# A four-batch attention and token-mixing kernel: another written-down order, split first reads, and Strassen pieces of 384 and 160 columns

## The chip, the cores and the metric

The kernel runs on one core of one Trainium2 chip. The core has five engines that run their own instruction streams in order and meet only at semaphores: TensorE (PE: matrix products and transposes), VectorE (DVE), ScalarE (ACT), GpSimd (POOL) and SyncE (SP), which here only starts transfers. Transfers are moved by 16 DMA engines; an engine that starts one spends some time on issuing it. The metric is the device time of one execution in microseconds (us), the median over several executions. Before the change it is 234.49 us (three runs, 233.85 to 238.21).

## The reference: what is computed

Two blocks follow each other, for a batch of B = 4, H = 4 heads, S = 1088 positions and head dimension D = 32, so that the model width is H*D = 128.

```python
def phi(x):                                   # r = 8 sketch directions
    a = np.einsum('rd,bhsd->bhsr', S1, x)
    b = np.einsum('rd,bhsd->bhsr', S2, x)
    return np.einsum('bhsi,bhsj->bhsij', a, b).reshape(*x.shape[:-1], r * r)
q_p, k_p = phi(q), phi(k)
kv  = np.einsum('bhsf,bhsd->bhfd', k_p, v)
num = np.einsum('bhsf,bhfd->bhsd', q_p, kv)
den = np.einsum('bhsf,bhf->bhs', q_p, k_p.sum(axis=2))[..., None] + 1e-6
x = num / den                                 # then heads side by side: (B, S, 128)
theta = x @ w_theta
zr, zi = x * np.cos(theta), x * np.sin(theta)
y = np.einsum('ts,bsd->btd', w_tok_r, zr) + np.einsum('ts,bsd->btd', w_tok_i, zi)
u = x + y
out = u + np.maximum(u @ w_ch, 0.0)
```

S1 and S2 are 8 x 32, w_theta and w_ch 128 x 128; these and the two 1088 x 1088 token matrices arrive as 64-bit floats and are turned into 32-bit ones on the chip. The denominator can come near zero, which is why the kernel works with split numbers (a rounded part and a rest) where the queries and keys meet.

## The kernel before

**Work per batch.** The 1088 positions are padded to nine chunks of 128, handled in three groups of three (384 columns). For the keys: the sum of squares on ScalarE (L676) sets a rounding step; VectorE writes the keys rounded to it (L700) and the rest of the subtraction (L705); TensorE forms the 32 x 32 second moments of rounded part and rest (L711 to L752). Beside this, `kfeatures` (L756) transposes the keys group by group (L779, the operation at L781), forms both sketches with the small matrix `sbk`, multiplies them out on VectorE and sums them against v. `chain` (L824) then turns the second moments into a small scaled matrix for the denominator: `split` on VectorE, an addition on ScalarE (L839), a product on TensorE (`first`, operands sq and sf), a split and a scaling (L867), a second product (operand pbd), and a row of some eleven tiny VectorE steps (`cut`) that ends in `mv` and `mf`. `levels` (L1020) multiplies the transposed queries with them (`exact` with 16-bit operands, `whole` with 32-bit ones), and VectorE makes the denominators. `outputs_x` (L1075) makes the attention output x, its angles and z, the 17 blocks of 128 rows (real and imaginary) that are mixed. The chains run for batch 0, batch 1, and batches 2 and 3 together.

**Mixing.** The token matrices come as 17 rows of 128 x 1088 64-bit numbers (1088 KB each). `weight` (L631) reads one into one of five buffers of class zs, makes two passes on ScalarE (L638, L640), and a shift and a combination on VectorE (L642, L644, the latter the custom operation on 128 x 2176 16-bit words). Batches 0 and 1 multiply every row by z directly, in pieces of 384, 384 and 320 columns (`mix_row`, L1208). Batches 2 and 3 are done together by Strassen's scheme (`winograd`, L1248): seven products of eight matmuls, each over half the positions (HT = 544 columns) that are cut into the pieces of PARTS (L149). The additions of rows that the scheme needs run on VectorE (asum 1 and 2) and on GpSimd (asum 3 and 4, in 16 operations of 128 x 544).

**End of a piece.** `finish` (L1234) multiplies u by w_ch on TensorE, adds the positive part on VectorE (L1238), transposes on VectorE (L1239) and stores the piece with four transfers, one for each 32 columns of the output, on SyncE's queue (L1241 to L1246).

**What sets the order.** No scheduler decides at build time. All operations are recorded first, each with its engine, its buffers and its readers and writers. Then `ORDER` (L34) gives the sequence in which they are issued, and `STARTS` (L79) a time for each. `run` (L245) uses the times to give buffers their slots, and `issue` (L264) uses them for one more thing: ahead of a TensorE operation it puts idle matmuls into TensorE's stream (`spin`, 128 x 384 with 16-bit operands), five for each microsecond that the written times leave between two TensorE operations:

```python
for _ in range(int((o.start - last - 0.08) * FILL)):
    fill()
```

Each engine then works through its own part of the order and waits wherever an operand or a buffer isn't ready. Besides these, 39 short idle matmuls of 112 columns open TensorE's stream (L430). Small transfers have no queue of their own: `read_heads` (L440) reads the two sketch matrices into the four heads' partitions, two of the four copies on ScalarE's queue and two with S2 alone on SyncE's, ahead of the keys.

Of the kernel before, what the change touches and what calls it, by code (L numbers as in the profile page):

```python
# [34 lines left out]
    4, 2, 5, 6, 0, 1, 3, 33, 30, 35, 7, 31, 8, 340, 137, 11, 9, 350, 12, 37, 13, 36, 14, 132, 34, 10, 21, 136, 335,  # L35
    48, 95, 138, 125, 96, 52, 370, 250, 53, 97, 15, 54, 49, 16, 231, 345, 251, 89, 232, 141, 142, 143, 254, 90, 119,
    17, 252, 55, 98, 133, 126, 56, 256, 57, 58, 59, 120, 60, 61, 62, 63, 64, 65, 26, 101, 75, 99, 66, 67, 144, 145,
    91, 102, 257, 50, 134, 76, 233, 18, 341, 77, 92, 139, 342, 140, 27, 78, 343, 42, 351, 68, 51, 69, 32, 70, 28, 71,
    19, 72, 255, 103, 344, 73, 227, 74, 121, 79, 29, 228, 93, 80, 243, 104, 244, 229, 81, 22, 352, 303, 82, 305, 122,
    353, 375, 83, 304, 20, 84, 41, 123, 161, 23, 146, 307, 85, 354, 86, 306, 308, 113, 87, 147, 234, 162, 336, 148,  # L40
    237, 114, 371, 127, 309, 88, 179, 163, 238, 245, 128, 310, 198, 420, 253, 423, 164, 180, 129, 421, 109, 424, 202,
    338, 135, 426, 425, 105, 427, 108, 44, 239, 43, 373, 428, 365, 315, 204, 422, 259, 258, 39, 94, 246, 191, 240,
    429, 346, 311, 430, 260, 100, 115, 45, 316, 431, 312, 106, 348, 376, 185, 432, 149, 150, 207, 46, 186, 433, 107,
    187, 230, 116, 337, 378, 151, 152, 153, 313, 434, 117, 154, 355, 261, 155, 314, 156, 262, 157, 158, 203, 159, 435,
    110, 192, 160, 436, 367, 193, 165, 181, 372, 437, 111, 438, 347, 112, 360, 118, 317, 263, 124, 439, 130, 166, 380,
    194, 167, 182, 208, 357, 446, 440, 442, 168, 188, 447, 441, 449, 131, 209, 453, 169, 443, 170, 450, 374, 448, 319,
    47, 456, 454, 318, 457, 199, 451, 455, 200, 377, 458, 171, 349, 444, 459, 390, 320, 339, 476, 445, 172, 452, 264,
    265, 361, 173, 468, 460, 478, 210, 470, 266, 267, 211, 268, 212, 269, 462, 270, 271, 461, 205, 356, 526, 174, 520,
    272, 463, 395, 366, 235, 523, 24, 527, 464, 175, 471, 521, 465, 479, 201, 25, 466, 241, 524, 176, 472, 469, 528,
    467, 40, 213, 236, 206, 525, 273, 274, 275, 242, 358, 522, 276, 485, 381, 529, 379, 480, 482, 359, 486, 474, 473,  # L50
    363, 391, 487, 530, 475, 277, 481, 362, 368, 488, 531, 410, 247, 177, 364, 214, 215, 278, 477, 489, 532, 392, 369,
    385, 490, 483, 396, 533, 178, 534, 491, 383, 382, 195, 405, 492, 384, 535, 386, 183, 323, 493, 324, 189, 285, 387,
    494, 536, 388, 400, 537, 321, 389, 248, 407, 216, 184, 38, 217, 218, 219, 190, 538, 220, 397, 221, 196, 484, 222,
    223, 224, 495, 393, 286, 415, 546, 225, 322, 394, 401, 549, 547, 226, 398, 197, 496, 402, 539, 249, 283, 548, 399,
    542, 284, 406, 287, 540, 288, 497, 550, 553, 289, 551, 541, 408, 556, 552, 403, 290, 543, 557, 404, 568, 544, 291,
    325, 554, 545, 292, 498, 409, 555, 417, 293, 560, 558, 562, 412, 499, 570, 563, 559, 299, 571, 411, 294, 660, 326,
    654, 576, 564, 561, 565, 413, 661, 572, 414, 655, 573, 657, 566, 658, 578, 567, 416, 500, 656, 418, 574, 579, 577,
    631, 419, 580, 632, 582, 633, 662, 585, 659, 569, 663, 501, 664, 665, 575, 608, 508, 586, 666, 581, 514, 634, 667,
    502, 609, 515, 279, 584, 329, 668, 296, 587, 669, 635, 670, 327, 509, 588, 671, 636, 295, 672, 589, 687, 610, 280,
    583, 611, 673, 516, 612, 281, 688, 590, 282, 328, 300, 297, 330, 637, 298, 613, 503, 680, 614, 517, 615, 842, 331,  # L60
    689, 332, 333, 591, 690, 691, 638, 334, 719, 616, 840, 725, 518, 720, 681, 519, 722, 721, 726, 674, 692, 723, 727,
    839, 617, 724, 592, 693, 728, 639, 729, 301, 675, 730, 731, 640, 676, 677, 618, 732, 678, 679, 593, 733, 302, 641,
    734, 619, 735, 594, 736, 694, 737, 682, 738, 642, 683, 752, 684, 696, 620, 685, 739, 595, 686, 702, 697, 745, 698,
    740, 699, 704, 596, 746, 741, 742, 643, 700, 705, 644, 743, 759, 744, 695, 747, 701, 597, 748, 749, 753, 621, 750,
    751, 706, 763, 844, 622, 843, 765, 710, 766, 845, 754, 712, 708, 713, 623, 755, 756, 767, 598, 818, 772, 645, 774,
    599, 768, 775, 600, 776, 707, 510, 777, 799, 757, 800, 758, 714, 703, 760, 624, 646, 761, 808, 601, 511, 771, 647,
    709, 762, 780, 801, 715, 764, 790, 648, 802, 769, 781, 778, 770, 819, 783, 791, 836, 803, 841, 773, 809, 784, 602,
    792, 779, 785, 793, 603, 787, 711, 512, 820, 649, 837, 513, 625, 847, 786, 804, 716, 821, 848, 717, 856, 805, 868,
    822, 857, 846, 806, 894, 865, 823, 858, 849, 850, 870, 851, 810, 718, 852, 807, 782, 896, 504, 788, 885, 869, 859,
    626, 794, 838, 795, 895, 866, 886, 853, 811, 824, 871, 825, 789, 796, 897, 860, 797, 861, 887, 873, 854, 862, 936,  # L70
    812, 798, 855, 863, 874, 902, 604, 971, 505, 888, 872, 876, 930, 864, 898, 605, 813, 606, 912, 877, 506, 814, 934,
    650, 913, 900, 815, 651, 867, 878, 899, 889, 875, 879, 816, 932, 890, 880, 817, 901, 933, 891, 652, 892, 653, 903,
    937, 828, 881, 829, 904, 939, 893, 507, 882, 931, 914, 941, 915, 883, 607, 954, 938, 884, 905, 935, 627, 945, 940,
    946, 830, 972, 955, 831, 956, 947, 942, 916, 826, 957, 827, 958, 944, 628, 948, 906, 943, 949, 959, 917, 832, 918,
    833, 960, 961, 950, 962, 951, 629, 919, 834, 630, 907, 984, 967, 952, 968, 908, 973, 985, 953, 909, 969, 974, 970,
    920, 975, 921, 963, 976, 835, 964, 977, 965, 978, 910, 966, 979, 911, 926, 922, 986, 923, 980, 927, 987, 924, 981,
    928, 982, 929, 988, 983, 989, 990, 994, 925, 991, 995, 992, 996, 993, 997, 998, 999, 1000, 1001,
)
STARTS = (  # L79
    90, 92, 103, 103, 130, 170, 220, 228, 274, 318, 360, 364, 389, 408, 454, 473, 473, 499, 510, 544, 560, 588, 592,  # L80
    622, 634, 648, 693, 742, 750, 764, 766, 782, 799, 872, 885, 893, 910, 924, 925, 988, 1016, 1019, 1030, 1034, 1036,
    1067, 1082, 1098, 1132, 1134, 1136, 1143, 1146, 1151, 1171, 1185, 1201, 1203, 1217, 1218, 1249, 1250, 1251, 1253,
    1255, 1257, 1257, 1259, 1261, 1263, 1265, 1278, 1284, 1305, 1296, 1330, 1355, 1368, 1381, 1383, 1398, 1403, 1417,
    1442, 1460, 1461, 1476, 1477, 1478, 1544, 1587, 1589, 1602, 1664, 1678, 1712, 1718, 1726, 1734, 1755, 1750, 1768,
    1771, 1781, 1783, 1795, 1807, 1808, 1816, 1834, 1835, 1846, 1876, 1914, 1965, 1963, 2007, 2028, 2031, 2042, 2043,
    2064, 2107, 2118, 2130, 2134, 2146, 2166, 2164, 2199, 2256, 2258, 2270, 2271, 2292, 2292, 2307, 2315, 2323, 2341,
    2369, 2397, 2412, 2410, 2421, 2445, 2448, 2496, 2510, 2542, 2560, 2545, 2575, 2568, 2607, 2622, 2678, 2717, 2731,
    2758, 2792, 2794, 2826, 2827, 2827, 2866, 2871, 2881, 2890, 2894, 2930, 2988, 2998, 2998, 3011, 3022, 3076, 3085,
    3113, 3134, 3141, 3171, 3178, 3181, 3202, 3218, 3246, 3253, 3265, 3288, 3302, 3309, 3330, 3335, 3359, 3346, 3347,
    3361, 3382, 3406, 3405, 3409, 3428, 3439, 3458, 3489, 3491, 3536, 3525, 3537, 3546, 3586, 3616, 3613, 3635, 3661,  # L90
    3678, 3711, 3713, 3720, 3745, 3745, 3774, 3784, 3799, 3802, 3812, 3827, 3841, 3879, 3886, 3892, 3912, 3905, 3942,
    3962, 3950, 3968, 3970, 3975, 3977, 3984, 3986, 3992, 3995, 4024, 4030, 4038, 4050, 4070, 4078, 4089, 4108, 4145,
    4171, 4199, 4213, 4285, 4305, 4309, 4318, 4323, 4350, 4343, 4382, 4384, 4410, 4416, 4419, 4433, 4441, 4456, 4464,
# [52 lines left out]
KEEP_CLS = "big"  # L146
PAIR = (2, 3)
QUADS = (2, 3)
PARTS = ((0, 288), (288, 544))  # L149
APOOL = ("4", "3")  # L150
KDMA = (False, True, True, True)
RDMA = (False,) * 4
# [24 lines left out]
class Layout:  # L177
# [17 lines left out]
    def buf(self, cls, shape, dt, name):  # L195
        b = Buf(cls, shape, dt, name)
        self.bufs.append(b)
        return b
# [1240 lines left out]
```

## Time and profile before

| | |
|---|---|
| median of three runs | 234.49 us (233.85 to 238.21) |
| the profiled execution's own time | 235.7 us |
| its span (first to last instruction) | 233.9 us |
| mean granted TensorE clock | 0.963 |
| PE busy | 222.1 us (95%), 2407 instructions |
| PE weight loads | 169.6 us (72%) |
| DVE busy | 178.9 us (76%), 364 |
| ACT busy | 112.8 us (48%), 239 |
| POOL busy | 54.5 us (23%), 99 |
| HBM read / written | 28.07 MB / 2.23 MB |
| share of the chain that ended last | PE 85%, ACT 5%, DVE 3%, DMA 2% |

A matmul with 32-bit operands appears as two records in the trace. Ends of matmuls are modelled, so a busy PE isn't a PE at its peak; the granted clock tells at which speed it streams. A line number in a row is that of the code before the change; L375, L379, L382 and L395 are helpers that many places call, so such rows are told apart by their tiles (ps is PSUM, big, zs, g, sm and hf are classes of buffers).

### The profile page before, as it was taken

Reading aid. Unit: us, or ns where it says so; the run is one execution under the profiler, and the core shown is the slowest. Engines: PE = TensorE matmul, PEld = TensorE weight load, DVE = VectorE, ACT = ScalarE, POOL = GpSimd, SP = SyncE. Lnnn points to the kernel's source line nnn. Section 1 sums busy time; section 2 is a strip of 40 time slices with the busy share of each in tenths; the row PEclk is TensorE's granted clock in tenths of the full one; section 3 lists DMA queues with packets and bytes.
Section 4 is the critical chain, followed back from the end, with each engine's and each line's share of the span. In section 5 each row is a group of like instructions: output and inputs, shape, how many; then the busy total and the mean of one; then the engine's idle time right before and its main releaser. Section 6 shows DMA issues by size and latency. Waiting matters only on the chain.

```text
span 233.9 us, 5837 instructions
## 1 busy us (share of the span) xinstructions
PE 222.1 (95%) x2407; PEld 169.6 (72%) x2407; DVE 178.9 (76%) x364; ACT 112.8 (48%) x239; POOL 54.5 (23%) x99
## 2 busy tenths in 40 slices
PE   7887999999999999999999999999999999999990
PEld 7665789877785667577766676677788878788770
DVE  3797586899999999999798789892678697534451
ACT  3895673999997647859842131555640000000000
POOL 1089052000470000001043000000025527980000
PEclk9999656999999999999999999999999999999996
DMA  4999999869585869400012210000051200522243
GB/s 143 417 406 300 423 416 379 317 252 425 204 296 123 304 247 308 181 0 4 0 28 34 36 28 3 3 3 4 0 72 23 34 3 0 87 35 33 43 72 54
DMA packets 24586, 33.55 MB, mean 143 GB/s; under 512 B 19184, under 2 KB 19952, under 8 KB 22384
## 3 DMA queue, kind: packets, MB, share of 16 engines
q1 hardware_dynamic: 23168, 30.29, 38.1%
q0 software_dynamic: 1296, 2.88, 6.1%
q8 instruction: 19, 0.31, 0.5%
q14 instruction: 7, 0.06, 0.1%
q10 hardware_dynamic: 96, 0.01, 0.0%
HBM read 28.07 MB, written 2.23 MB: 130 GB/s over the span
## 4 chain that ended last, share of the span: by engine, by line
PE 85%; ACT 5%; DVE 3%; DMA 2%; issue 2%; SPq 1%; DVEq 0%; ACTq 0%
PE ps L395 76%; ACT big L640 2%; PE ps L779 2%; PE ps L1005 2%; DMA big<-k_l 2%; PE ps L427 2%; PE ps L1151 2%; PE ps L1118 1%; DVE big L375 1%; ACT big L676 1%; ACT g L782 1%; DVE g L1239 0%; DVE big L382 0%; DVE g L375 0%; ACT g L1122 0%
## 5 line engine op out<-in xcount | busy, mean ns | idle before, releaser
L395 PE MATMUL ps<-big,zs 128*128 128x384 f32 (+3 forms) x380 | 112.8, 437 | 0.0
L395 PEld LDWEIGHTS ps<-big,zs 128*128 128x128 f32 x380 | 69.7, 190 | 27.0 <-DVE mv L379 0.6
L375 POOL TENSOR_TENSOR big<-big,big 128x544 f32<-128x544 f32 x16 | 22.4, 1420 | 13.3 <-PE ps L395 8.6
L640 ACT ACTIVATE big<-zs 128x1088 int32<-128x1088 uint32 (+1 forms) x18 | 21.2, 1196 | 4.8 <-DVE big L375 2.5
L638 ACT ACTIVATE big<-zs 128x1088 f32<-128x1088 f32 x17 | 21.0, 1234 | 4.7 <-DMA zs<-w_tok 3.8
L395 PE MATMUL ps<-big,big 128*32 128x32 f32 (+2 forms) x352 | 23.2, 234 | 0.0
L375 DVE CUSTOM_DVE_ANT_0 big<-big,big 128x2176 uint16<-128x2176 uint16 x17 | 21.8, 1290 | 0.1
L395 PEld LDWEIGHTS ps<-big,big 128*32 128x32 f32 (+1 forms) x352 | 16.7, 125 | 3.3 <-issue 0.3
L389 POOL DMA_DIRECT2D g<-big x6 | 5.3, 940 | 55.7 <-ACT g L1228 55.7
L427 PE MATMUL ps<-idle 128*128 128x112 bf16 (+1 forms) x78 | 13.4, 333 | 2.3 <-POOL idle L429 1.3
L375 DVE TENSOR_TENSOR zs<-ps,g 128x768 f32<-128x768 f32 (+2 forms) x20 | 12.6, 629 | 3.6 <-ACT g L1166 3.0
L379 DVE TENSOR_SCALAR big<-big 128x1088 int32<-128x1088 int32 x17 | 12.1, 719 | 0.5 <-ACT big L638 0.5
L395 PE MATMUL ps<-sbk,g 128*128 128x64 f32 x72 | 11.2, 300 | 0.3 <-ACT g L782 0.2
L395 PEld LDWEIGHTS <-hf 128*32 128x32 bf16 (+1 forms) x252 | 9.0, 100 | 3.4 <-issue 2.3
L375 DVE TENSOR_TENSOR g<-lv 128x768 f32<-128x768 f32 x12 | 11.2, 951 | 0.1
L395 PEld LDWEIGHTS ps<-sbk,g 128*128 128x128 f32 x72 | 10.3, 215 | 1.3 <-issue 0.7
L395 PEld LDWEIGHTS ps<-w,big 128*128 128x128 f32 x72 | 9.4, 191 | 2.2 <-ACT big L1131 0.7
L375 DVE TENSOR_TENSOR big<-big,hf 128x1152 f32<-128x1152 f32 x8 | 10.9, 1361 | 0.1
L427 PEld LDWEIGHTS <-idle 128*128 128x128 bf16 x78 | 7.8, 132 | 4.2 <-issue 1.5
L382 DVE SCALAR_TENSOR_TENSOR big<-ps,big 128x288 f32<-128x288 f32 (+1 forms) x8 | 3.4, 440 | 9.5 <-PE ps L395 9.5
L379 POOL TENSOR_SCALAR sm<-sm,ec 128x4 f32<-128x4 f32 x4 | 2.1, 518 | 35.4 <-DVE sm L375 35.2
L395 PE MATMUL ps<-w,big 128*128 128x128 f32 x72 | 10.1, 279 | 0.1
(197 smaller groups left out, 380.5 us busy)
## 6 DMA issues: line engine op xcount, KB each, us to landing
zs<-w_tok SPq DMA_DIRECT2D x17, 1088.0 KB, 6.8
big<-k_l SPq DMA_DIRECT2D x7, 576.0 KB, 6.0
big<-q_l SPq DMA_DIRECT2D x4, 576.0 KB, 12.1
big<-v_l SPq DMA_DIRECT2D x4, 576.0 KB, 10.3
big<-hf POOLq DMA_DIRECT2D x3, 576.0 KB, 5.7
g<-big POOLq DMA_DIRECT2D x4, 192.0 KB, 3.0
out<-g SPq DMA_DIRECT2D x16, 48.0 KB, 1.8
out<-g SPq DMA_DIRECT2D x16, 36.0 KB, 1.7
```

The lines of the kernel that those rows point to most:

```text
L375: eng.tensor_tensor(out=o, in0=a, in1=b, op=f)
L379: (eng or V).tensor_scalar(out=o, in0=a, scalar1=s1, scalar2=s2, op0=op0, **kw)
L382: (eng or V).scalar_tensor_tensor(out=o, in0=a, scalar=s, in1=b, op0=op0, op1=op1)
L389: op("G", 0.9, lambda: G.dma_start(dst(), src(), accum_op=ALU.add), w, r, fly=fly)
L395: T.matmul(o, lhs, rhs, start=start, stop=stop, skip_group_check=True)
L427: T.matmul(nowhere()[:, :n], idle()[:, 0:P], idle()[:, :n], start=True, stop=True, skip_group_check=True)
L638: op("A", 0.22 + n * 0.0009, lambda: A.activation(dfn(), words_of(raw(), n)[1].bitcast(F32), AF.Prelu, scale=2.0**-112, alpha=-(2.0**32)), ...
L640: op("A", 0.22 + n * 0.0009, lambda: A.activation(stp(), words_of(raw(), n)[0].bitcast(U32), AF.Copy, scale=2.0**-29), [stp], [raw])
L676: op("A", act(n) + 0.1, lambda: A.activation(flat(r()), kc(), AF.Square, accum_out=km()[:, 1:2]), [r, (km, 1)], [kx])
L779: T.transpose(tr()[:, i * P:(i + 1) * P], kx()[:, g * GC + i].rearrange("p h d -> p (h d)"), ident())
L1005: T.transpose(tr()[:, i * P:(i + 1) * P], x()[:, g * GC + i].rearrange("p h d -> p (h d)"), ident())
L1151: T.transpose(x()[:, i], xs()[:, off + i * P:off + (i + 1) * P], ident())
```

## The change

Six edits, none of which changes what is computed:

1. `ORDER` and `STARTS` are written anew, nearly from the first entry. The kernel before reads the keys of batches 1, 0 and 3 first, the kernel after those of 0, 1 and 3; w_sq comes 5th among the large reads (before it was 14th), and v of batch 0 is the 13th (before the 15th). Ahead of the first real matmul stand 5 and 6 idle matmuls of 384 columns, with the small transpose of L482 between them; before, 11 stood behind it. Behind these there are 32 idle matmuls of 384 columns instead of 28. Each engine still has the same operations apart from the edits below.
2. The keys of batch 0 are read in three transfers of 384 columns.
3. Their transposes in `kfeatures` depend on the transfer of their own group alone.
4. The sketch matrices are read by ScalarE's queue alone: four copies and S2. The S2 transfer reuses the completion semaphore of the first key transfer and is issued only when that has landed; behind it on ScalarE are the table load and everything else.
5. PARTS is 384 and 160 columns instead of 288 and 256.
6. The pieces of batches 2 and 3 are stored by two queues, two transfers on SyncE's and two on ScalarE's.

```diff
 ORDER = (
-    4, 2, 5, 6, 0, 1, 3, 33, 30, 35, 7, 31, 8, 340, 137, 11, 9, 350, 12, 37, 13, 36, 14, 132, 34, 10, 21, 136, 335,
...
+    4, 2, 29, 5, 0, 31, 1, 30, 34, 36, 3, 32, 43, 35, 38, 6, 7, 341, 351, 10, 8, 138, 11, 9, 49, 12, 20, 53, 37, 133,
...
-PARTS = ((0, 288), (288, 544))
+PARTS = ((0, 384), (384, 544))
...
-        op("A", 0.48 * 2, lambda: read_heads(A, 0, 2), [(st, 0)], [], due=-4000.0, fly=2.7)
-        op("S", 0.1, lambda: read_heads(SY, 2, H), [(st, 1)], [], due=-4000.0, lk=3)
+        op("A", 0.44 * (H + 1), lambda: read_heads(A, 0, H), [(st, 0)], [], due=-4000.0, fly=1.45)
...
+        if b == 0 and nm == "k":
+            for g in range(NG):
+                c = slice(g * GC, (g + 1) * GC)
+                op("S", 192 * 1024 / 400e3, lambda c=c: SY.dma_start(t()[:, c], src[b][:, c]), [(t, g)], [], due,
+                   lead=LOAD_LEAD)
+            return
...
-            op("P", 0.33, trs, [tr], [kx], hold=[kT])
+            op("P", 0.33, trs, [tr], [(kx, g)], hold=[kT])
...
-        def store():
-            for f in range(DM // SQ):
-                SY.dma_start(out[b, t0:t0 + w, f * SQ:(f + 1) * SQ].rearrange("(c j) i -> j c i", j=SQ),
-                             ot()[f * SQ:(f + 1) * SQ, :w].rearrange("j (c i) -> j c i", i=SQ))
-
-        op("S", w * P * 4 / 100e3, store, [], [ot], due, lk=4)
+        def store(E, f0, f1):
+            for f in range(f0, f1):
+                E.dma_start(out[b, t0:t0 + w, f * SQ:(f + 1) * SQ].rearrange("(c j) i -> j c i", j=SQ),
+                            ot()[f * SQ:(f + 1) * SQ, :w].rearrange("j (c i) -> j c i", i=SQ))
+
+        if b in PAIR:
+            op("S", w * P * 2 / 100e3, lambda: store(SY, 0, 2), [], [ot], due, lk=2)
+            op("A", 0.92, lambda: store(A, 2, 4), [], [ot], due, fly=2.1)
+        else:
+            op("S", w * P * 4 / 100e3, lambda: store(SY, 0, DM // SQ), [], [ot], due, lk=4)
```

## The prediction

> **What bounds the kernel now.** Page first: the activity in 40 slices, 5.85 us each. The rows are TensorE, VectorE and the granted TensorE clock.
>
> ```profile
> PE   7887999999999999999999999999999999999990
> DVE  3797586899999999999798789892678697534451
> PEclk9999656999999999999999999999999999999996
> ```
>
> From slice 12 (about 68 us) to the end TensorE is at 9 and its clock full. VectorE is at 9 from slice 8 to 18. The clock is down in slices 5 to 7. So the kernel has two parts: up to the first mixing row, chains of waits and a clock loss; behind it, TensorE with no slack. A gain must come from an earlier mixing start, from less TensorE work, or from the tail. I next took windows around the clock's fall. Columns: length, then busy time (count) of PE, PE weight loads, DVE, ACT, POOL; then clock, DMA share, GB/s.
>
> ```profile
> 20.00:22.00 2.00, 1.80 (x35) 1.47 (x34) 1.84 (x5) 1.66 (x4) 2.00 (x7) 1.00 1.07 324
> 22.00:24.00 2.00, 0.10 (x1) 0.13 (x2) 0.85 (x4) 0.00 (x0) 1.59 (x8) 1.00 1.04 350
> 24.00:26.00 2.00, 1.94 (x27) 1.52 (x28) 0.83 (x4) 1.49 (x3) 0.00 (x0) 0.85 1.02 423
> 26.00:28.00 2.00, 2.00 (x11) 1.59 (x9) 1.59 (x3) 2.00 (x7) 0.00 (x0) 0.50 1.04 440
> ...
> 38.00:40.00 2.00, 2.00 (x21) 2.00 (x21) 1.11 (x2) 0.14 (x1) 0.44 (x1) 0.74 1.03 365
> ```
>
> TensorE does 0.10 us of work in 22 to 24; the clock halves inside 24 to 26 (mean 0.85 means 1.4 us at full, then half: the fall is at 25.4) and returns inside 38 to 40 (0.74: at 39.04). That is 13.64 us at half speed, so 6.8 us of full-speed work lost. Third, the timeline: start, duration, engine, line, tiles, and in brackets the idle time before and its releaser.
>
> ```profile
> 3.54 0.24 ACT L459 ACTIVATE sp<-st 128x48 f32<-128x48 f32 x1
> 6.12 1.16 ACT L676 ACTIVATE big<-big 128x1152 f32<-128x1152 f32 x1 [1.21 <-DMA big<-k_l]
> ...
> 23.90 0.52 PE L779 MATMUL ps<-ident,big 128*128 128x128 f32 x3 [1.93 <-DVE sm L379]
> ...
> 24.68 0.25 PE L395 MATMUL ps<-sq,sm 32*32 32x16 f32 x8
> ...
> 35.93 1.65 PE L395 MATMUL ps<-mv,hf 128*128 128x96 f16 x18
> ...
> 68.42 1.83 PE L395 MATMUL ps<-big,zs 128*128 128x384 f32 x5
> ```
>
> The square of the first keys (L676) starts at 6.12. Batch 0's denominator product (`first`, sq and sm) runs at 24.68; in TensorE's order it stands behind L779 transposes that had waited 1.93 us for VectorE. The first `exact` product is at 35.93 (read mv), the first mixing row at 68.42. The 60.87 us from TensorE's first real matmul (7.55) to there are idle 4.06, clock loss 6.8, 28 idle matmuls of 384 columns at 0.177 (11 took 1.95) = 4.96, and 45.05 of work.
>
> **The change, part by part.**
>
> *Small reads by ScalarE's queue* (edit 4). SyncE now starts with the keys: first issue about 1.0 instead of 2.26. Small reads land 1.7 to 1.9 us after issue; with 192 KB I put the first third's landing at 3.0 to 3.3. ScalarE's S2 issue waits for that, lands 1.9 later, and behind it queue the table load (1.28), L459, L471 and the squares: every first step of ScalarE. L459 moves from 3.54 to about 5.5, L482 from 4.95 to 6.85, the first real matmul from 7.55 to about 8.2, the first square from 6.12 to 6.8. Loss at the start 0.65; bounds 0.2 (landing at once behind the table) to 1.6 (a landing 1 us later). Idle matmuls cover TensorE's wait.
>
> *Three reads of the first keys* (edits 2, 3). In the new order TensorE's first real matmuls are transposes of batch 1's keys, one whole read, behind idle matmuls. So 0; bounds 0 and -1.0 (two thirds of a 576 KB read, which lands 1.4 us after the one before).
>
> *The order* (edit 1). Each engine keeps its operations, so the gain is in what waits. On batch 0's chain I summed rows: VectorE's work from its first rounding (0.90, then subtraction 1.27, outer products 0.86, shift 0.64, small steps 0.2) to batch 0's split is 12.2 us, from 9.1 to 21.3 (before 20.77). ScalarE's comes to 14.4, from 6.8 to 21.2, its addition to 21.6. So `first` can run at about 22.0 instead of 24.68, as no L779 group waits ahead of it. From there, with each new neighbour counted: second product about 25.1 (before 27.04), end of `cut` 29.65 (31.94), first `exact` 30.4 (35.93: 4.0 of other work, at half clock, stood between the two), levels on VectorE 35 (42.02). VectorE has 25 us of work from levels to z (24.96 before, when it had no idle time from 42.02 to 80): z at about 60.4. TensorE's own bound is 8.2 + 45.05 + 32 idle matmuls x 0.177 (5.66) + idle 3.5 = 62.4 if the clock isn't lost. So mixing starts at 62.4 at the earliest, 6.0 earlier than 68.42. Nothing of the trace prices the semaphore hops of a new order; VectorE's hop from product to step was about 0.4, and I take off 1.5 for some four of them: **-4.5** (bounds -6.0 and -0.7, if the clock is lost as before: 62.4 + 6.8 less 1.5 of waits that the slow work fills).
>
> The clock decides this. In the new order idle matmuls stand in TensorE's stream at about 13, 15.5 to 16.8 (7), 19.9 (3), 21.3 (6), 22.6 (4), 25.8 and 29; the longest stretch without is 3.1 us, where before there was none from 18.1 to 24.3. Its waits are shorter too: 1.55 by my sums (17.75 to 19.3, on VectorE's psc) against 1.93. A wait of 0.92 before 17.11 had left the clock at 1.00. So I take no fall. That the records say 2.00 of 2.00 busy in 26 to 28, at 0.50, shows that busy records don't bring the clock back by themselves. [...]
>
> *Mixing.* It is TensorE-bound, but the rows start earlier while ScalarE and VectorE, which prepare them (two passes of about 1.2, shift 0.7, combination 1.3 a row), are still busy with the chains; VectorE and ScalarE were full to about 68. The new order gives TensorE nine rows before more chain work. Stalls of 0 to 3; I take **+1.0**, by the sum of three small lateness gaps (1.6, 0.6 and 0.3) that the rows give, less what TensorE's other ready work hides.
>
> *384 + 160 columns* (edit 5). Both cuts stream 544. Before, 88 records of mean width 272 took 20.0 us (227 ns each, the streaming time), so no gaps. 160 columns stream in 0.133; the 128-column rows lie 0.107 to 0.12 apart, weight load included. At worst 0.013 x 128 = +1.6; I take 0. VectorE's finish steps scale with width and have idle there.
>
> *The tail* (edits 5, 6). TensorE's last large product ends at 227.35, and then:
>
> ```profile
> 227.42 0.39 DVE L375 TENSOR_TENSOR big<-big,ps 128x256 f32<-128x256 f32 x1
> 227.86 0.70 PE L395 MATMUL ps<-big,w 128*128 128x256 f32 x2 [0.51 <-DVE big L375]
> 228.60 0.42 DVE L382 SCALAR_TENSOR_TENSOR big<-ps,big 128x256 f32<-128x256 f32 x1 [0.79 <-PE ps L395]
> ...
> 229.06 0.45 DVE L1239 STREAM_TRANSPOSE g<-big 128x256 f32<-128x256 f32 x1
> ```
>
> Five-eighths of the columns: these four steps (1.96) lose some 0.6, scaled above a fixed part. Then SyncE issues four stores, 0.47 each, to 231.7, and 1.8 follow for data and end. With two issues on each queue, 0.95 goes. ScalarE has nothing left behind 172 us, so its half costs nothing. **-1.55** (bounds -1.0, if ScalarE's issues are the slower, and -1.8).
>
> **Sum.** -4.5 + 1.0 - 1.55 = -5.05; the start's loss is within the first term. The profiled execution took 235.7 (span 233.9 and 1.8 around it), so 230.65; it lay 1.2 above the median 234.49, so **229.4**.
>
> **Rivals.**
>
> *The clock falls all the same.* Its place is the wait before 19.3, or one of 22 to 26; it needs a wait near 1.9 us, which a start 0.4 later would give. For: the fall before came after 1.93; 1.55 is my sum. Against: the idle matmuls on both sides. [...]
>
> *TensorE starves in mixing.* In-order, it waits at a row whose combination VectorE hasn't made; VectorE is saturated from 42 to 80. For: nine rows in sequence. Against: rows need 3.4 us of ScalarE and VectorE each against 7.3 us of TensorE for 24 records. The price is the upper bound, +3 instead of +1, and one more such gap of 1.1: 232.5.
>
> [...]
>
> *The change doesn't do what it says* for the three reads: in the sum, at 0.
>
> **How the numbers follow.** Forecast 0.48 (229.4; own range 226.5 to 231.5, from the mixing bounds and the -6.0 end); clock falls 0.20 (232.3); starving 0.12 (232.5); slower 0.20 (237.5). 2%, 4.7 us, is about what a measurement of this kernel can tell from no change. Below 229.8 lies a little over half of the forecast's case and nothing much else: 0.30. Above 239.2 lies half of the last, with its long upper side: 0.10. Between them 0.60. The range reaches from 226.5 to 236.5, leaving out the upper part of the last rival and the low tail.
>
> **What would show it.** Right: PEclk full in slices 3 to 10; L459 near 5.5; the product of sq and sm near 22; `exact` near 30; the first mixing row (big, zs, 384 columns) near 63 to 64; TensorE without idle behind it; last product to span's end near 4.0 instead of 6.55 (227.35 to 233.9). Wrong: a slice with clock below 0.9; a first row after 66; rows of L395 with big,zs that show idle time released by VectorE; 160-column records above 0.15 us. The forecast is wrong most probably by the clock.

## The result and the profile after

The changed kernel is slower: 243.38 us (median of 4 runs, 241.72 to 244.37) against 235.61 us for the kernel before (4 runs, 233.85 to 238.21; 234.49 was the median of the first three). The ratio is 1.0348, with a 95% interval of 1.0238 to 1.0459. Ratios here and below leave out executions more than 1.5% above the fastest of their kernel, and medians leave out none. The forecast was 229.4, with a range to 236.5. The profiled execution has a span of 241.9 us, against 233.9.

The activity in 40 slices of the changed kernel (6.05 us each), as before: TensorE, VectorE and the granted TensorE clock.

```profile
PE   7598999999999997999999999999999659999991
DVE  1467799999999999698999699394976991235362
PEclk9687999999999999999999999999999967999998
```

Two things are new against the page before. TensorE has a dent at 5 in the second slice (6 to 12 us), and one at 6 and 5 in slices 32 and 33 (188 to 200 us), in the middle of what was a stretch without slack. The clock is down in both places, and full at 30 to 40 us, where it had been down before.

Next the rows that answer to those shown of before: start, duration, engine, line, operation and tiles, and in brackets the idle time before and its releaser (lines of the changed code).

```profile
3.18 0.52 ACTq L446 DMA_DIRECT2D st<-s  x1
7.68 0.24 ACT L459 ACTIVATE sp<-st 128x48 f32<-128x48 f32 x1 [2.46 <-DMA st<-s]
8.99 0.37 PE L482 MATMUL ps<-ident,m 128*2 128x128 f32 x1 [3.40 <-DVE m L501]
...
28.65 0.25 PE L396 MATMUL ps<-sq,sm 32*32 32x16 f32 x8
...
36.60 1.31 PE L396 MATMUL ps<-mv,hf 128*128 128x96 f16 x27
...
68.49 5.75 PE L396 MATMUL ps<-big,zs 128*128 128x384 f32 x18
```

L459 starts at 7.68 (before 3.54), `first` at 28.65 (24.68), the first `exact` at 36.60 (35.93), and the first mixing row at 68.49 (68.42). So the start lost 4 us and they were won back by the first mixing row, no more.

The end of the kernel, the same view:

```profile
236.43 0.32 DVE L376 TENSOR_TENSOR big<-big,ps 128x160 f32<-128x160 f32 x1 [0.26 <-PE ps L396]
236.80 0.54 PE L396 MATMUL ps<-big,w 128*128 128x160 f32 x2 [0.41 <-DVE big L376]
237.38 0.33 DVE L383 SCALAR_TENSOR_TENSOR big<-ps,big 128x160 f32<-128x160 f32 x1
237.74 0.35 DVE L1245 STREAM_TRANSPOSE g<-big 128x160 f32<-128x160 f32 x1
```

The last large product ends at 236.39 and the span at 241.9: 5.51, where it was 6.55. The 8.0 us between the spans are therefore 0.07 up to the first mixing row, 8.97 from there to the last large product (167.90 against 158.93), and -1.04 in the tail.

Where the 8.97 went is told by windows of five microseconds (length; busy time and count of PE, PE weight loads, DVE, ACT, POOL; clock, DMA share, GB/s) and by the waits of TensorE:

```profile
185.00:190.00 5.00, 5.00 (x24) 3.72 (x23) 3.70 (x6) 0.00 (x0) 4.78 (x5) 1.00 0.18 29
190.00:195.00 5.00, 1.44 (x7) 0.84 (x5) 5.00 (x1) 0.00 (x0) 5.00 (x5) 1.00 0.07 10
195.00:200.00 5.00, 3.58 (x6) 2.09 (x7) 4.89 (x10) 0.00 (x0) 0.75 (x2) 0.54 0.14 23
200.00:205.00 5.00, 5.00 (x16) 3.17 (x16) 0.67 (x2) 0.00 (x0) 1.09 (x1) 0.78 0.12 20
```

```profile
PE ps L396 <- DVE big L383: 5.0, 1, 5.0
PE ps L482 <- DVE m L501: 3.4, 1, 3.4
PE ps L396 <- issue: 1.5, 1, 1.5
```

In 190 to 195 VectorE is busy 5.00 of 5.00 with one single instruction. TensorE waits 5.0 us for VectorE's next one (L383), which is to empty a PSUM piece; then the clock halves (0.50 within the windows whose means are 0.54 and 0.78), which costs 3.41 us of work (the sum of one minus the clock over windows of 1 us; about 0.5 of it falls while TensorE still waits). Idle time from 68.49 on is 6.47, these 5.0 and a wait of 1.5 at 93. The long instruction on VectorE, and what GpSimd does meanwhile:

```profile
187.18 1.26 DVE L376 TENSOR_TENSOR big<-big 128x544 f32<-128x544 f32 x1
188.37 7.38 DVE L376 TENSOR_TENSOR big<-big 128x544 f32<-128x544 f32 x1
195.67 0.60 DVE L383 SCALAR_TENSOR_TENSOR big<-ps,even,big 128x384 f32<-128x384 f32 x1
```

```profile
186.53 1.33 POOL L376 TENSOR_TENSOR big<-big,big 128x544 f32<-128x544 f32 x1
187.81 0.85 POOL L390 DMA_DIRECT2D g<-big  x1
188.42 1.61 POOL L376 TENSOR_TENSOR big<-big,big 128x544 f32<-128x544 f32 x1
189.72 1.60 POOL L376 TENSOR_TENSOR big<-big,big 128x544 f32<-128x544 f32 x1
...
193.59 1.57 POOL L376 TENSOR_TENSOR big<-big,big 128x544 f32<-128x544 f32 x1
```

An addition of asum 2 takes 7.38 us. Every other VectorE addition of 128x544 takes at most 0.73, except the one just before it (1.26). The long one ends 0.6 after GpSimd's fifth addition in a row (193.59 + 1.57 = 195.16). Both engines read two operands from SBUF. I took it that GpSimd's additions kept VectorE's out. A wait for one of them would be 1.3 us (they start 1.30 apart, at 188.42 and 189.72); here it is five.

### The profile page after: what moved, and what is told of

The parts are those of the page before. It is cut to its first block, busy times and chain, and to the rows that moved or that the text cites. A ratio compares the mean times of both kernels' runs of the same rounds, so it can differ in the third digit from the quotient of the medians.

```text
span 241.9 us, 5860 instructions
## 1 busy us (share of the span) xinstructions
PE 223.4 (92%) x2411; PEld 160.9 (67%) x2411; DVE 181.4 (75%) x364; ACT 112.4 (46%) x239; POOL 62.1 (26%) x99
## 4 chain that ended last, share of the span: by engine, by line
PE 83%; DVE 8%; issue 3%; DMA 3%; ACT 1%; DVEq 0%
PE ps L396 73%; DVE big L376 4%; PE ps L428 2%; PE ps L785 2%; DMA st<-s 2%; PE ps L1124 2%; PE ps L1157 2%; PE ps L1011 1%; DMA big<-k_l 1%; ACT big L640 1%; DVE sm L380 1%; DVE sm L383 1%; DVE big L380 1%; DVE sm L376 0%; DVE big L383 0%
## 5 line engine op out<-in xcount | busy, mean ns | idle before, releaser
L396 PE MATMUL ps<-big,zs 128*128 128x384 f32 (+2 forms) x380 | 113.4, 443 | 6.5 <-DVE big L383 5.0
L396 PEld LDWEIGHTS ps<-big,zs 128*128 128x128 f32 x380 | 66.5, 192 | 39.3 <-issue 8.2
L376 POOL TENSOR_TENSOR big<-big,big 128x544 f32<-128x544 f32 x16 | 21.6, 1438 | 16.2 <-issue 11.6
L390 POOL DMA_DIRECT2D g<-big x6 | 5.3, 926 | 63.8 <-ACT g L1234 63.8
L428 PE MATMUL ps<-idle 128*128 128x384 bf16 (+1 forms) x82 | 14.7, 337 | 1.3 <-POOL idle L430 1.3
L376 DVE TENSOR_TENSOR big<-big 128x544 f32<-128x544 f32 x8 | 12.9, 1618 | 0.4 <-PE ps L396 0.4
L383 DVE SCALAR_TENSOR_TENSOR big<-ps,even,big 128x384 f32<-128x384 f32 (+1 forms) x10 | 4.8, 494 | 9.2 <-PE ps L396 9.2
L380 POOL TENSOR_SCALAR mf<-mv 128x32 f32<-128x32 f16 x4 | 1.2, 302 | 36.5 <-DVE mv L380 36.5
L1049 ACT COPY lv<-ps 128x480 f32<-128x480 f32 x12 | 6.6, 555 | 8.3 <-PE ps L396 8.1
L396 PE MATMUL ps<-sbk,g 128*128 128x64 f32 x72 | 9.7, 276 | 0.0
L396 PE MATMUL ps<-mf,big 128*128 128x96 f32 x72 | 9.5, 279 | 0.2 <-DVE big L376 0.2
```

Of the source, the lines that this page charges most:

```text
L376: eng.tensor_tensor(out=o, in0=a, in1=b, op=f)
L380: (eng or V).tensor_scalar(out=o, in0=a, scalar1=s1, scalar2=s2, op0=op0, **kw)
L383: (eng or V).scalar_tensor_tensor(out=o, in0=a, scalar=s, in1=b, op0=op0, op1=op1)
L390: op("G", 0.9, lambda: G.dma_start(dst(), src(), accum_op=ALU.add), w, r, fly=fly)
L396: T.matmul(o, lhs, rhs, start=start, stop=stop, skip_group_check=True)
L428: T.matmul(nowhere()[:, :n], idle()[:, 0:P], idle()[:, :n], start=True, stop=True, skip_group_check=True)
```

## The experiments

Three questions: is the early loss the late S2, is the 5 us wait the meeting of VectorE and GpSimd, and what is the rest of the change worth?

**The small reads.** First the small reads of edit 4 are given to two queues again, with SyncE's share behind the first third of the keys:

```diff
-        op("A", 0.44 * (H + 1), lambda: read_heads(A, 0, H), [(st, 0)], [], ...)
+        op("A", 0.44 * (H + 1), lambda: (read_heads(A, 0, 2), read_heads(SY, 2, H)), [(st, 0)], [], ...)
```

> The changed kernel with edit 4 undone: two copies of the sketch matrices by ScalarE's queue, two and S2 by SyncE's, behind the first third of the keys; all else as changed. Theory: S2, issued at 3.18 behind a landing of a key transfer, came at 7.65 because the DMA engines were already full of key reads; with it issued by about 2 us, L459 starts near 3.6 to 4.2 instead of 7.68, L482 near 5 to 5.5 instead of 8.99, the clock holds at the start, and the first mixing row comes 3 to 4.5 us earlier than 68.49 (64 to 65.5). The 5 us stall near 191 stays if it comes from VectorE and GpSimd, so the time is about 239 to 240. Rival (the start is hidden behind other waits): first mixing row at 67.5 to 68.5 and 243.

Measured: 240.92 us, ratio 1.0174 (1.0064 to 1.0284) to the kernel before. S2 is issued at 2.10 and L459 starts at 4.31; L482 comes at 6.23, the first mixing row at 66.07, 2.4 earlier than in the changed kernel. The 5.0 us wait stays. So early reads bring L459 early, as expected. The gain at the mixing start is smaller than the 3 to 4.5 expected, and it isn't shown to come from them: this profile lost 1.70 us of clock before mixing, the changed kernel's 5.12. More on this under the table.

Then the keys of batch 0 are one transfer again and the small reads stay on ScalarE, so that S2 need not wait for a key transfer's semaphore:

```diff
-                op("S", ..., lambda c=c: SY.dma_start(t()[:, c], src[b][:, c]), [(t, g)], [], due, ...)
+                op("S", ..., lambda c=c, g=g: SY.dma_start(t().rearrange("p c h d -> p (c h d)"),
+                    src[b].rearrange("p c h d -> p (c h d)")) if g == 0 else None, [(t, g)], [], due, ...)
```

> The changed kernel with batch 0's keys in one transfer again (edits 2 and 3 undone), the small reads still all on ScalarE's queue. S2 then needs no completion semaphore of a key transfer and is issued at about 2.8. If the late landing (4.5 us after its issue) came from waiting for that semaphore, S2 lands near 4.7 and L459 starts near 4.9. If it came from standing behind key reads in full DMA engines, S2 still lands 3 to 4.5 after its issue and L459 starts at 6 to 7.3. Total by the first 240 to 241, by the second 241.5 to 243.

Measured: 242.35 us, ratio 1.0248 (1.0114 to 1.0381). Its ScalarE rows:

```profile
3.03 0.61 ACTq L446 DMA_DIRECT2D st<-s  x1
8.10 0.24 ACT L459 ACTIVATE sp<-st 128x48 f32<-128x48 f32 x1 [2.92 <-DMA st<-s]
```

S2 is issued at 3.03 with no such wait and still comes 5.1 us later. So the semaphore isn't what makes it late: it goes out when the key transfers are under way (the DMA share is 0.97 in 5 to 10 us of the changed kernel). Issued at 1.87 (before) or 2.10 (above), the same 2 KB are there 1.7 to 2.2 us later. S2 isn't alone in this: L459 needs the four copies of 4 KB too. In the changed kernel they are issued at 0.98 to 2.36, beside the keys, and land 2.3, 3.4, 3.3 and 4.9 us later, the last at 7.29 (before: 1.7 to 1.9 us later).

**VectorE against GpSimd.** Asum 3 and 4 go to VectorE, in the same places of the order (`APOOL = ()` instead of `("4", "3")`):

> The changed kernel with the sixteen row additions that GpSimd makes (asum 3 and 4) on VectorE, in the same places of the order; so no GpSimd additions run between 185 and 219. Theory: the addition of 128x544 that took from 188.4 to 195.8 on VectorE was locked out by five GpSimd additions back to back; here all 544 additions take about 0.72, the 5.0 us wait of TensorE near 191 and the clock loss behind it (about 2.7) go, and VectorE's 16 x 0.72 = 11.5 more work has room: 235 to 237.5. Rival (the addition waited for something else, a semaphore or a buffer): one addition of 7 us stays, and the time is 243 to 246.

Measured: 233.44 us, ratio 0.9829 (0.9699 to 0.9959). No addition of 128x544 takes over 0.73, the 5 us wait and the clock loss behind it are gone, and the stretch from the first mixing row to the last product is 158.61 instead of 167.90. The long addition was a matter of GpSimd. (It is 7.38 in the profiles of the two runs above too.) But is it any run of GpSimd additions? The kernel before has one of nine, from 197.2 on. Three additions that nothing reads were put on VectorE beside it:

```diff
+                x = rows[NK - 1]()
+                for n in (384, 544, 384):
+                    tt(V, held()[:, :n], x[:, :n], x[:, HT:HT + n], ALU.add)
```

> The kernel before with three additions that nothing reads put into VectorE's stream behind the transpose at 197.8, where it idles and GpSimd runs nine additions back to back (197.2 to 209.5): 128x384, 128x544, 128x384, both operands in SBUF. If an addition is let in at each end of a GpSimd addition, each takes at most 1.34 + its own 0.55 to 0.72. If a run of GpSimd additions keeps VectorE out to its end, the first takes up to 11 us. If only the wide form is kept out, the 384 ones take under 1.9 and the 544 one up to 9.

They took 0.74, 1.74 and 1.57 (one execution, 234.76 us): each was let in when the GpSimd addition in progress ended. So a run as such keeps nobody out, and my explanation was too simple. What differs? In the changed kernel the long one follows another addition directly. Two experiments on that:

> The kernel before with three additions that nothing reads behind the transpose at 197.8, as in the run before, but each with an output of its own, so that VectorE has no semaphore between them (384, 544, 512 columns), while GpSimd adds. In the run before, with a semaphore between, each was let in at the next end of a GpSimd addition. If VectorE additions that follow each other with nothing between are what is kept out (as the second of the two at 187.2 and 188.4 in the changed kernel), the second and third wait for the end of the run of GpSimd additions: 5 to 10 us. If not, each takes at most 1.9.

Without a semaphore between them they took 0.75, 1.85 and 1.82 (one execution, 234.11 us). The second, and the GpSimd addition whose end let it in:

```profile
196.54 1.85 DVE L375 TENSOR_TENSOR lv<-big 128x544 f32<-128x544 f32 x1
196.16 1.65 POOL L375 TENSOR_TENSOR big<-big,big 128x544 f32<-128x544 f32 x1
```

The pair isn't it. And in the changed kernel the long addition was moved behind the step that frees PSUM (shown as VectorE's sequence before and after the edit of the order):

```diff
-    DVE: add 128x544, add 128x544 (the long one), L383 384, L383 320, add 128x544
+    DVE: add 128x544, L383 384, add 128x544 (the long one), L383 320, add 128x544
```

> The changed kernel with one VectorE instruction moved: the addition of 128x544 that took from 188.4 to 195.8 is put behind the step that frees the PSUM piece TensorE waits for (one operand in PSUM), so it no longer follows another addition of its kind directly. If the pair is what was kept out, the addition takes at most 2.1, and TensorE's 5.0 us wait and the clock loss behind it go: 236 to 238. If a run of five GpSimd additions keeps every VectorE addition out, it still takes 5 to 7, but the step ahead of it is free and TensorE's wait falls to 1 to 3: 238 to 241.

It took 8.14, now through six GpSimd additions. TensorE's wait fell from 5.0 to 2.2, because the step it waits for went ahead. The two executions took 235.04 and 238.85 us. So the run keeps VectorE out here also when no other addition stands directly ahead; that points to GpSimd. There the run follows a transfer issue (L390 at 187.81). That issue was put ahead of GpSimd's first addition, and nothing else was changed (GpSimd's sequence):

```diff
-    POOL: add, add, L390 transfer issue, add, add, add, add, add
+    POOL: L390 transfer issue, add, add, add, add, add, add, add
```

> The changed kernel with GpSimd's transfer issue that stands between its second and third addition (187.8) put ahead of the first: so the additions from 188.4 on no longer follow a transfer issue directly. Measured so far: additions behind that issue start 1.29 apart though each takes 1.6, and keep VectorE's 128x544 addition out for five or six of them; in the kernel before, additions that follow a wait take 1.34, start 1.30 apart, and let VectorE in at every end. Theory (the transfer issue makes GpSimd's instructions overlap, so the place is never free): no VectorE addition over 2.1, TensorE's 5.0 us wait goes, 236 to 238.5. Rival (it is the run of additions or their operands): an addition of 5 to 9 us stays, and 241 to 244.

Measured: 235.41 us, ratio 1.0012 (0.9963 to 1.0062), against 1.0348 with the issue in its old place. The addition at issue, and GpSimd beside it:

```profile
189.64 1.86 DVE L382 TENSOR_TENSOR big<-big 128x544 f32<-128x544 f32 x1
```

```profile
189.10 1.81 POOL L382 TENSOR_TENSOR big<-big,big 128x544 f32<-128x544 f32 x1
```

It takes 1.86; no other takes more. The stretch from the first mixing row to the last product is 160.65, with no clock lost in it. In its new place the issue starts at 181.55, and GpSimd then stands idle, so that no addition follows it directly:

```profile
186.50 1.34 POOL L382 TENSOR_TENSOR big<-big,big 128x544 f32<-128x544 f32 x1 [3.75 <-issue]
```

The opposite was done to the kernel before: the three additions again, and on GpSimd one transfer of 128x160 that nothing reads, behind the first of the nine additions:

```diff
+    L.extra = lambda: G.dma_start(held()[:, 1280:1440], rows[NK - 1]()[:, :160])
```

> The kernel before with the three additions that nothing reads (384, 544, 352 columns, nothing between them) on VectorE behind the transpose at 197.8, and a transfer of 128x160 that nothing reads, issued by GpSimd behind the first of its nine additions: what the run without the transfer let in at every end of an addition (0.75, 1.85, 1.82). If a transfer issue directly ahead keeps VectorE out, one of the three takes 6 to 11 us, and GpSimd's additions start 1.29 apart at 1.6 each. If not, each stays under 2.2.

Measured: 248.37 us (one execution). GpSimd and VectorE there:

```profile
200.36 0.61 POOL L1240 DMA_DIRECT2D lv<-big  x1
200.98 10.34 POOL L379 TENSOR_TENSOR big<-big,big 128x544 f32<-128x544 f32 x8
```

```profile
200.08 0.75 DVE L379 TENSOR_TENSOR lv<-big 128x384 f32<-128x384 f32 x1
200.75 11.15 DVE L379 TENSOR_TENSOR lv<-big 128x544 f32<-128x544 f32 x1
```

The 544 addition waits for all eight GpSimd additions, 11.15 us instead of 1.85, and TensorE waits 8.5 for VectorE. One transfer issue directly ahead of the run turns the one case into the other, in both kernels. The expectation was wrong in a detail: I had taken the 1.6 us of GpSimd's additions for the sign of it, and here they take 1.32 to 1.35 while VectorE is out all the same. Why an issue does this is open. So is whether it is the issue itself or a transfer that is still on its way when the run begins. By the traces the transfer landed at 190.80 in the changed kernel and at 202.44 here, well before either run of additions ended, but with the issue moved it had landed at 185.08, before the first addition.

**What the rest is worth.** The tail edits alone, in the kernel before:

```diff
-PARTS = ((0, 288), (288, 544))
+PARTS = ((0, 384), (384, 544))
-                SY.dma_start(out[b, t0:t0 + w, ...
+                (A if b in PAIR and f > 1 else SY).dma_start(out[b, t0:t0 + w, ...
```

> The kernel before with edits 5 and 6 alone: pieces of 384 and 160 columns, and the stores of batches 2 and 3 by two queues. From the end of the last large product to the end of the span 5.0 to 5.5 instead of 6.55 (the changed kernel has 5.5); the time 0.5 to 1.5 below the kernel before, so same. Rival: the other piece widths shift VectorE's additions against GpSimd's as in the changed kernel, and an addition of 128x544 over 5 us appears: 3 to 7 above.

Measured: 236.42 us, ratio 1.0032 (0.998 to 1.0083). From the last large product to the end it takes 5.49, as expected, but a gain of 1.06 can't be seen in the time. No long addition appears.

Small reads undone and the additions on VectorE together:

> The changed kernel with edit 4 undone (small reads by two queues) and the sixteen additions of asum 3 and 4 on VectorE: both suspected losses taken away, the new order, the three reads, 384 + 160 columns and two-queue stores kept. Theory: first mixing row at 62.5 to 66 as the prediction's sum had it, no wait of 5 us near 190, clock full or lost for one window at the start: 229 to 233, 0.97 to 0.985 of the kernel before. Rival (the gain of the order is used up by VectorE's extra 11.5): 234 to 237.

Measured: 234.11 us, ratio 0.9993 (0.9953 to 1.0032). Expected was 0.97 to 0.985. First mixing row at 67.46; in its profile TensorE waits 2.0 us for a key transfer. The one window of lost clock in this expectation, and in that on the filled wait below, is 3.41 us at half clock, as the profile of the changed kernel has it from 21.29 to 24.70. Early small reads gained nothing here: with the additions on VectorE alone the ratio is 0.9829, and 0.9926 in the repeat below. Then the clock was tried by itself, in the kernel before, with eleven idle matmuls in the wait of 1.93 us:

```diff
+                if L.nth == 7:
+                    for _ in range(11):
+                        spin()
```

> The kernel before with eleven idle matmuls of 384 columns (1.95 us) ahead of the transposes at 23.9, in the 1.93 us in which TensorE waits there. Theory: that wait is what loses the clock (6.8 us of work at half speed); with it filled, the clock stays full in the profile or loses one window, the first mixing row comes at 64 to 66 instead of 68.4, and the median falls by 1 to 4. Rival: other waits near 15 to 17 or the transposes themselves lose it as often, and the time is the same within 1.

Measured: 234.70 us, ratio 1.0018 (0.999 to 1.0047). The clock of 12 of its 13 executions was 0.978 to 0.995, where that of the kernel before was 0.966 to 0.989 in 20 of 29 and 0.941 to 0.956 in the rest, and the time did not move. The thirteenth is the profiled one (0.961, 238.85 us). There the wait before 23.9 is gone, and the clock falls at 17.1 us, after a wait of 1.0, and at 54.7, after one of 1.15. And more idle matmuls at the start of the changed kernel (70 for 39), with the additions on VectorE:

> The changed kernel with the sixteen additions on VectorE, and 70 instead of 39 idle matmuls of 112 columns at the start, which reach to about 8.1 where TensorE waited from 5.6 to 9.0 for the late S2. Theory: no clock loss at the start, first mixing row at 64 to 65, 229.5 to 232.5: 0.975 to 0.99 of the kernel before. Rival (the later waits lose the clock as often): 232 to 235, no difference from the kernel before.

Measured: 236.86 us, ratio 1.0095 (1.0055 to 1.0134), slower than the same kernel with 39 (above and below). Expected was 0.975 to 0.99. The clock of its executions was 0.975 to 0.996, not below that of the kernel before, so what makes it slower is open. Last, both suspected faults taken away with no work moved to VectorE, and the additions on VectorE once more, side by side on one chip:

> The changed kernel with both faults taken away and no addition moved to VectorE: the small reads by two queues, and GpSimd's transfer issue ahead of its first addition. What is left of the change is the order, the three reads, the piece widths and the stores. If the prediction's term for the order (-4.5) was right apart from the two faults, first mixing row at 63 to 65 and 229 to 232 (0.975 to 0.99 of the kernel before). If the order brings nothing at the same clock loss, first mixing row at 65.5 to 68.5 and 233 to 236 (0.995 to 1.005).

> The changed kernel with the sixteen additions on VectorE once more, in more executions: before, 233.4 at a ratio of 0.983 (0.970 to 0.996) in four executions, with a profile that lost no clock. If that gain is of the kernel, 0.975 to 0.99 again; if it was the clock of those executions, 0.995 to 1.01.

Measured: 233.97 us for both (12 executions each), ratios 0.9946 (0.9906 to 0.9986) and 0.9926 (0.9872 to 0.998). Both are faster than the kernel before by about half a per cent. The profile of the first loses no clock before the first mixing row and reaches it at 66.71. `first` is at 25.04, not at 22.0. Two ScalarE rows of it show waits that the sum didn't have:

```profile
9.30 1.17 ACT L688 ACTIVATE big<-big 128x1152 f32<-128x1152 f32 x1 [2.47 <-DMA big<-k_l]
...
19.83 1.21 ACT L644 ACTIVATE big<-zs 128x1088 f32<-128x1088 f32 x1 [1.95 <-DMA zs<-w_tok]
```

Some of these profiles by their parts (clock loss: the sum of one minus the clock, in us, over windows of 1 us):

| profile | first mixing row | clock loss before it | from there to the last product | tail | span |
|---|---|---|---|---|---|
| before | 68.42 | 6.83 | 158.93 | 6.55 | 233.9 |
| before, with probes from 196.6 | 66.58 | 1.71 | 159.81 | 6.61 | 233.0 |
| before, with the second probes (195.9) | 65.98 | 1.71 | 159.78 | 6.54 | 232.3 |
| changed | 68.49 | 5.12 | 167.90 | 5.51 | 241.9 |
| changed, small reads undone | 66.07 | 1.70 | 168.53 | 5.60 | 240.2 |
| changed, small reads undone, additions on VectorE | 67.46 | 1.71 | 160.05 | 5.78 | 233.3 |
| changed, small reads undone, issue moved | 66.71 | 0.00 | 159.64 | 5.65 | 232.0 |
| changed, issue moved | 68.93 | 5.12 | 160.65 | 5.62 | 235.2 |
| changed, long addition moved | 65.30 | 0.00 | 162.47 | 5.53 | 233.3 |
| changed, additions on VectorE (first) | 64.27 | 0.00 | 158.61 | 5.82 | 228.7 |
| changed, additions on VectorE (second) | 64.81 | 0.00 | 159.74 | 5.75 | 230.3 |

The last four rows and the row "changed" have the same instructions up to the start of mixing, and in all five S2 is late (L459 at 6.82 to 8.32). Two of them lose 5.12 us of clock and start mixing at 68.49 and 68.93. Three lose none and start at 64.27 to 65.30, earlier than any profile with early small reads (66.07 to 67.46). So the late S2 by itself isn't shown to cost anything at the mixing start; what differs among the five is the clock. Nor do the times settle what early reads are worth: the ratio with them is 1.0174 against 1.0348, and 0.9946 against 1.0012 with the issue moved, but 0.9993 against 0.9829 and 0.9926 with the additions on VectorE.

## Why the prediction was wrong

The sum was -4.5 (order, start within it) + 1.0 (mixing) - 1.55 (tail) = -5.05. By the profiles it is 0.07 + 8.97 - 1.04 = 8.0.

- **Mixing, +1.0, measured +8.97.** This is the step that failed most. It spoke of starving rows only, and took the new order's effect on VectorE against GpSimd for nothing. A wait of 1.5 at 93 is within the 0 to 3 that it allowed; the profile names no releaser, so that it was for a row isn't shown. The rest is one addition of 7.38 us, which made TensorE stand still for 5.0 us, and the clock loss of 3.41 behind that; the runs show that it hangs on one GpSimd transfer issue standing directly ahead of five additions. Moving that issue alone takes the time from a ratio of 1.0348 to 1.0012. I had listed each engine's operations as unchanged, and looked at GpSimd's queue for nothing but lateness.
- **The start, loss 0.65 (bounds 0.2 to 1.6), measured 3.5 at the first real matmul** (11.07 for 7.55; I had 8.2), and 4.0 at L482 (8.99 for 4.95; I had 6.85). The 1.9 us from issue to landing came from small reads issued ahead of the key reads. S2 went out behind key transfers and took 4.5; with it issued early, L459 comes at 4.31. The wait of 3.40 us that followed went with a fall of the clock at about 8 us, which the sum had excluded. It isn't the rule: with the long addition moved, the same wait took 3.65 and no clock was lost.
- **The order, -4.5.** It rested on busy times of VectorE and ScalarE added up without a wait for transfers. With both suspected faults gone and no clock lost, `first` stands at 25.04 instead of 22.0; ScalarE waits 2.47 and 1.95 for transfers, in its order, with the DMA share at 0.92 to 1.04 from 5 to 25 us. A part of my gain was also none of the kernel's: the 6.83 of clock loss in the profile of before. Where the changed start lost no clock, mixing began at 64.27 to 65.30, close to the 63 to 64 that I had written down; the sum set a start that holds its clock against one that had lost it. In the last comparison, executions of the kernel before had spans of 231.5 (mean clock 0.987) and of 235.0 (0.962). The two probe kernels are the kernel before up to 195 us, lost 1.71, and start mixing at 65.98 and 66.58. Against these the new order starts 0.7 to 2.3 earlier with late small reads and no clock lost (64.27 to 65.30), and between 0.5 earlier and 1.5 later with early ones (66.07 to 67.46). So at a low clock loss the term lies between about -2.3 and +1.5, and part of the -2.3 is the 1.71 that the probe kernels lost.
- **The tail, -1.55, measured -1.04** (bounds -1.0 to -1.8). Right in kind.
- **384 + 160 columns, 0.** Right: with both suspected faults gone, the stretch of mixing is 159.64 against 158.93.
- **Three reads, 0.** With one read again the time is 242.35 (2 executions) against 243.38, so nothing speaks for a gain.
- **The rivals.** The two times set on the clock, 232.3 and 237.5, rest on my estimates of a fall that lasts shorter or longer than the 13.64 of the profile before, which no row of that profile shows; in the table the loss before the first mixing row is 0.00 to 6.83. The clock did fall early, at 7.6 and 21.3 us, with 5.12 lost, but that is no more than the 6.83 of the profile before. The main loss was in no rival. My chance of 0.10 for slower by over 2% was too small mostly because I looked for trouble where the profile of before had shown some.

The clock: I took the 1.93 us wait for what loses it. Filling that wait raised the clock of most executions and left the time at 1.0018. Nor does a fall need a wait near 1.9: in the changed kernel the one at 21.3 came after a wait of 0.81. The same kernel loses more or less from run to run (the executions of the kernel before have 0.941 to 0.989); why wasn't shown. A loss before mixing is also partly hidden in waits: 0.987 to 0.962 is 5.8 us of 232, and the two spans above differ by 3.5.

## What to carry to other kernels

When an order changes, read which additions it puts side by side on VectorE and GpSimd, and what stands directly ahead of each run, also on an engine that is far from the bound: here one transfer issue in GpSimd's stream cost 3% of the kernel (1.0348 against 1.0012). Time a small transfer by what was issued ahead of it (2 KB took 1.7 to 2.2 us to its reader when issued at about 2 us here, 3.6 to 5.1 when issued at 3.0 to 3.2 behind the key reads), not by how long such transfers took elsewhere. And don't book a clock loss of one profiled execution as the kernel's own before other executions show it.

## What the runs showed of the hardware

- GpSimd additions (128x544, both operands in SBUF) in a row let a VectorE addition in at each end: 0.74 to 1.86 us for what takes 0.52 to 0.72 alone (the kernel before with either set of probes; the changed kernel with the issue moved). Directly behind a transfer issue on GpSimd they didn't: 7.38 through five (in three profiles), 8.14 through six, 11.15 through eight (the kernel before with the added transfer). That time stands inside the VectorE instruction, in a row that names no releaser, so the engines don't meet at semaphores alone. What the issue changes inside GpSimd wasn't seen in any run.
- VectorE's instructions with one operand in PSUM were not kept out: for 256 to 384 columns 0.42 to 0.55 beside such additions in the kernel before (197.36 to 208.5), 0.56 and 0.62 in the changed one (211.03 and 213.78, 384 columns), against 0.45 to 0.55 with GpSimd idle (before, 187.87 to 190.3).
- A transfer of 2 KB took 1.7 to 2.2 us to its reader when issued at about 2 us (the kernel before, and the changed one with the small reads undone), and 3.6 to 5.1 when issued at 3.0 to 3.2 behind 1152 or 1728 KB of key reads, with or without a semaphore to wait for.
- The clock losses in the table are 0.00, 1.70 to 1.71, 5.12 and 6.83. Before the tail the clock stood at half for 13.64 us in the profile of before (from 25.4), and for 6.83, 3.41 and 6.83 in that of the changed kernel (from 7.64, 21.29 and 195.37). During TensorE waits of 3.40 and 3.97 ahead of L482 the clock fell (the changed kernel, and the one with the issue moved), during one of 3.65 it didn't (long addition moved).
